# One fixed order for all five engines: a planner that orders by due times replaced by a written table

## The chip, the cores and the metric

The kernel runs on one core of a Trainium2 chip. The metric is device time in microseconds (us); lower is better. Inputs and output are float32 in device memory; the kernel computes in float16 with float32 accumulation.

## The reference

Retention (a linear attention with a decay per head) over four sequences, and then a two-layer network with GELU on its output:

```python
# q, k, v: (B=4, H=8, S=768, D=64)
gamma = 1 - 2 ** (-5 - arange(H))
for t in range(S):
    state = gamma * state + outer(k[t], v[t])          # per batch and head, 64 x 64
    y[t]  = q[t] @ state / 8
x   = y.transpose(0, 2, 1, 3).reshape(3072, 512)       # tokens x (heads * 64)
out = gelu_tanh(x @ w_in) @ w_out                      # w_in 512 x 2048, w_out 2048 x 512
```

## The kernel before

The sequence is cut into six chunks of 128 positions. A chunk holds four batches `b` = 0 to 3, so 512 tokens. All work is named by chunk and batch or by chunk and part.

**Attention of a chunk**, on the tensor engine (PE), per batch: `T` transposes the scaled q and k (L211; from chunk 3 on, q is transposed by DVE instead), `A` makes the 128 by 128 products of k and q (L220), `Yc` adds what the state of the chunks before contributes (L239), `Y` the products with v (L251), and `S` the new state (L262). Between them DVE and ScalarE (ACT) take results out of PSUM: `evT` (a copy), `evA` (times a mask, L271), `evY` (the chunk's `x`, L278 or a copy), `evS` (the state, L283). Before that, q, k and v of a batch are cast or scaled from float32 to float16 (L161, L159, L176), on ACT, DVE or GpSimd (POOL). The scaling of v from chunk 2 on is one instruction for each batch, on POOL or DVE.

**The network.** For chunk 0 and 1, `M1` is the plain product with `w_in` (L357), GELU on ACT (L373), and for chunk 0 `M2` the plain product with `w_out` (L515, 16 pieces of four matmuls of 512 columns). From there on both products use seven block products in place of eight (`m1w` L492, `m2w` L504): they need sums of halves of the operands (L394): `xs` (four sums of the chunk's x, on POOL), `gs` (16 sums of the activations, on POOL or DVE, tile `s_g`) and sums of the weights (DVE, once). Results in PSUM are combined by ACT copies (`snap`, L159) and DVE additions (`add`, L394).

**Order.** The first 34 us are written out by hand: chunk 0's attention, with `spin` matmuls on zeros (L135) where PE has nothing, then M1 of chunk 0. Chunk 0's M1 runs as three pairs of weight columns over batches 0 and 1, then 2, then 3, and ten full-width pieces of 512 columns. The weights are loaded by GpSimd's queue, four parts of `w_in` and four of `w_out`, each 512 KB as it lands in float16. In the hand-written part:

```python
    load_w_in(0)
    prep1(PO, "k", 0, 2)
    for i in range(1, 4):
        load_w_in(i)
    prep1(PO, "k", 0, 3)
    prep1(PO, "q", 0, 3)
    for i in range(NO):
        load_w_out(i)
```

Everything after that is put in order by a greedy planner inside the kernel: every operation has its needs, the engines that may run it with a duration for each (`KIND`), and a slack; at each step the planner starts the operation that can start first on any engine by its own clock. PE's work stands in four threads (attention, two of M1, M2). Engines execute their instructions in the order in which they were emitted, so the planner's choice is final. PSUM's eight banks are handed out in that order too.

The loads of q, k and v come through the queues of SyncE (SP) and ACT. Those of chunk 1 are held back until the GELU of piece 12 of M1 of chunk 0.

Of the kernel before, what the change touches and what calls it, by code (L numbers as in the profile page):

```python
# [12 lines left out]
ALU = mybir.AluOpType  # L13


@with_exitstack
def kernel(
# [9 lines left out]
    nc = tc.nc  # L27
# [93 lines left out]
    load1(nc.sync, "k", 0, 2)  # L121
    load1(nc.sync, "q", 0, 3)
    load1(nc.sync, "v", 0, 3)

# [7 lines left out]
    def spin(n):  # L132
        ps = bank("h", shape=(128, 512), name="spin_ps")
        for _ in range(n):
            nc.tensor.matmul(  # L135
                out=ps, lhsT=zero[:, 0:128], rhs=zero, start=True, stop=True
            )
# [180 lines left out]
    def o_S(b, tag="att"):  # L318
        pss["S", b] = bank(tag, shape=(128, NHP, 64), name="s_ps")
        mm_s(0, b, pss["S", b])  # L320

    def o_evS(b, eng=nc.vector):
        copy_on(eng, st_of(b), pss.pop(("S", b)))


# [48 lines left out]

    def moe1(c, fc):
        h_ps = bank("h", shape=(128, B * C), name="h_ps")
        moe1_mm(c, fc, h_ps, 0, B * C)
        gelu(g_tile(c, fc)[:, fc % 2], h_ps)

    def moe1_two(c, fp, t0, t1):  # L380

        h_ps = bank("h", shape=(128, 2, B * C // 2), name="h_ps")
        for r in range(2):
            moe1_mm(c, 2 * fp + r, h_ps[:, r, 0:t1 - t0], t0, t1)
        gelu(g_tile(c, 2 * fp)[:, :, t0:t1], h_ps[:, :, 0:t1 - t0])
# [145 lines left out]
    load1(AC, "q", 0, 2)  # L531
    load1(AC, "v", 0, 2)
    spin(14)
    prep1(VE, "q", 0, 0)
    prep1(PO, "k", 0, 0)
    prep1(AC, "v", 0, 0)
    o_T(0)
    o_evT(0, AC)
    load1(AC, "k", 0, 3)
# [4 lines left out]
    o_evA(0)  # L544
    o_T(1)
# [4 lines left out]
    o_S(0, "o")  # L550
    o_evY(0, AC)
    prep1(VE, "q", 0, 2)

    load_w_in(0)
    prep1(PO, "k", 0, 2)
    for i in range(1, 4):
        load_w_in(i)
    prep1(PO, "k", 0, 3)
    prep1(PO, "q", 0, 3)
    for i in range(NO):  # L560
        load_w_out(i)
    o_A(1)
    o_evA(1)
    spin(3)
    o_T(2)
    o_evT(2, AC)
    spin(2)
    o_Y(1)
    o_S(1, "o")
    o_evY(1, AC)  # L570
    prep1(AC, "v", 0, 2)
    spin(2)
    o_A(2)
    o_evA(2)
    o_evS(0, AC)
    prep1(AC, "v", 0, 3)
    o_evS(1, AC)
    spin(6)
    o_T(3)
    o_evT(3)  # L580


    t01, t2, t3 = (0, half), (half, half + C), (half + C, 2 * half)
    moe1_two(0, 0, *t01)
    o_A(3)
    o_evA(3)
    o_Y(2)
    o_S(2)
    o_evY(2, AC)
    moe1_two(0, 1, *t01)  # L590
    o_evS(2)
    moe1_two(0, 0, *t2)
    moe1_two(0, 1, *t2)
    o_Y(3)
    o_S(3)
    o_evY(3)
    o_evS(3)
    moe1_two(0, 2, *t01)
    for fp in range(2):
        moe1_two(0, fp, *t3)  # L600
    moe1_two(0, 2, half, 2 * half)

    raw["q", 1, 0] = tile_of(*LD1[0], shape=SIZE["ld"][1])
    ld_at["q", 1, 0] = LD1.pop(0)
    for fc in range(6, NF):
        moe1(0, fc)
        if fc == 12:
            nc.scalar.copy(out=raw["q", 1, 0][0:1, 0, 0:1], in_=g_tile(0, 10)[0:1, 0, 0:1])
    for bs in ((0, 1), (2, 3)):
        for b in bs:  # L610
            load1(SY, "q", 1, b)
            load1(SY, "k", 1, b)
        for b in bs:
            load1(SY, "v", 1, b)
    nc.sync.dma_start(out=dec.rearrange("p h t -> p (h t)"), in_=dec_h.ap())

    ENG = {"ACT": AC, "DVE": VE, "POOL": PO, "SP": SY}
    KIND = {
        "gelu": {"ACT": (0.51, 0.60)},
        "snap": {"ACT": (0.51, 0.59)},  # L620
        "add": {"DVE": (0.62, 0.70)},
        "evA": {"DVE": (0.61, 0.69)},
        "evY": {"DVE": (0.61, 0.69)},
        "evY1": {"ACT": (0.51, 0.59), "DVE": (0.61, 0.69)},
        "evS": {"DVE": (1.10, 1.20)},
        "evT": {"DVE": (0.62, 0.69), "ACT": (0.92, 1.01)},
        "cast": {"ACT": (0.53, 0.62), "POOL": (0.58, 0.62)},
        "cast2": {"ACT": (1.06, 1.15), "POOL": (1.18, 1.22)},
        "trq": {"DVE": (0.60, 0.69)},
        "evTk": {"DVE": (0.36, 0.44), "ACT": (0.50, 0.58)},  # L630
        "loadq": {"SP": (8.6, 0.0)},
        "scale": {"POOL": (1.00, 1.05), "DVE": (0.68, 0.75)},
        "scale1": {"POOL": (1.00, 1.05), "DVE": (0.68, 0.75)},
        "sumg": {"POOL": (1.12, 1.16), "DVE": (0.35, 0.42)},
        "sumx": {"POOL": (1.12, 1.16)},
        "sumw": {"DVE": (0.35, 0.42)},
        "sume": {"POOL": (1.12, 1.16), "DVE": (0.35, 0.42)},
        "load": {"SP": (0.90, 0.0)},
        "store": {"SP": (0.80, 0.0)},
    }  # L640
    LAT_PE, LAT, SAFE, AHEAD = 0.28, 0.07, 1.5, 0.4
    tok, T = {}, {}
    slots = {p: [0.0] * n for p, (n, _, _) in SIZE.items()}
    slots["bank"] = [0.0] * 8
    held_by = {}
    free_at = {"PE": 34.2, "ACT": 34.7, "DVE": 25.0, "POOL": 21.0, "SP": 47.5}
    landed = [48.6, 49.6, 51.5, 52.4]
    port = [0.0]
    todo, by_need = [], {}

    class Op:
        def __init__(self, kind, emit, needs, gives, alloc=(), free=(), slack=1.0, early=(), kb=0):
            self.kind, self.emit, self.needs, self.gives = kind, emit, needs, gives
            self.alloc, self.free, self.slack, self.early, self.kb = alloc, free, slack, early, kb

    def shared(o, e):

        return e == "POOL" or e == "DVE" and o.kind[:3] in ("sum", "sca")

    def op(*a, **k):  # L660
        todo.append(Op(*a, **k))

    def when(needs):
        t = 0.0
        for n in needs:
            if n not in tok:
                return None
            t = max(t, tok[n])
        return t

    def room(alloc):

        t, seen = 0.0, {}
        for off, (key, *_) in alloc:
            seen.setdefault(key[0], []).append(off)
        for p, offs in seen.items():
            at = sorted(x for x in slots[p] if x is not None)
            if len(at) < len(offs):
                return None
            t = max(t, max(a - o for a, o in zip(at, sorted(offs))))  # L680
        return t

    def take(alloc):
        for key, readers, *shape in alloc:
            p = key[0]
            i = min((x, i) for i, x in enumerate(slots[p]) if x is not None)[1]
            if p == "lq" and key[2] in BLK:
                i = key[3]
            slots[p][i] = None
            held_by[key] = [p, i, readers, 0.0]  # L690
            T[key] = bank_tile(i, *shape) if p == "bank" else tile_of(p, i)

    def give_back(keys, t):
        for key in keys:
            h = held_by[key]
            h[2] -= 1
            h[3] = max(h[3], t)
            if h[2] == 0:
                slots[h[0]][h[1]] = h[3]

    def finish_op(o, e, s):
        busy, lat = KIND[o.kind][e]
        free_at[e] = s + busy
        end = s + lat + LAT
        if shared(o, e):
            port[0] = s + busy
        if e == "SP":
            begin = max(landed[-1], s + 1.3)
            landed.append(max(begin + 1.15 * o.kb / 256, s + busy + 1.8 if o.kind == "loadq" else 0.0))
            end = landed[-1] + SAFE  # L710
            free_at[e] = max(free_at[e], landed[-4] if o.kind == "load" else 0.0)
        take(o.alloc)
        o.emit(ENG[e])
        for n in o.early:
            tok[n] = s
        for n in o.gives:
            tok[n] = end
        give_back(o.free, end)


    def ld_key(c, b, nm):
        early = c == 2 and b < 2 and nm != "v" or c in BLK and nm == "q"
        return ("lq" if early else "ld", nm, c, b)

    def q_cast(c, b):
        key = ("qk16", c, b)

        def emit(eng):
# [8 lines left out]
           alloc=[(key, 2 if c + 1 == NCk else 3)], early=[("al", key)], free=[("lq", "q", c, b)], slack=2.0)  # L737

        def tr(eng):
# [7 lines left out]
           early=[("al", "qkT", c, b)], free=[key], slack=1.5)  # L747

    def q_load(c):
# [3 lines left out]
        def emit(eng):  # L753
# [8 lines left out]
           early=[("issued", key)], slack=3.0, kb=1024)  # L762
        prev[0] = ("issued", key)

    def cast_in(c, b, nm):
# [4 lines left out]
        ldk = ld_key(c, b, nm) if c > 1 else ("ld", nm, c, b)  # L770
# [8 lines left out]
        if nm == "v":  # L779
            kind = "cast" if c < 2 else "scale"  # L780
        elif kind == "scale":
            kind = "scale1"
# [7 lines left out]
            slack=8.0 if nm == "v" else 2.0,  # L790
        )

    prev = [None]
# [14 lines left out]
    def sub(cost, emit, needs=(), gives=(), alloc=(), free=()):  # L808
        return (cost, emit, list(needs), list(gives), list(alloc), list(free))

    def att(c):
        units = []

        def T1(b):
# [498 lines left out]
```

## Time and profile before

| What | Value |
|---|---|
| Time, median of 3 runs | 204.42 us (204.28 to 204.44) |
| The profiled execution | 204.52 us, its span 202.7 us, so 1.8 us lie outside the span |
| Granted TensorE clock | 0.998 |
| PE busy | 192.5 us (95%) |
| DVE busy | 150.5 us (74%) |
| ACT busy | 126.6 us (62%) |
| POOL busy | 96.6 us (48%) |

A span is the time from the first to the last instruction. A busy share is an average over stages; PE also counts as busy on `spin` matmuls, which compute nothing. The tables by stretch of time that follow tell more than these shares.

### The profile page before, as it was taken

Reading aid. Unit: us, or ns where it says so; the run is one execution under the profiler, and the core shown is the slowest. Engines: PE = TensorE matmul, PEld = TensorE weight load, DVE = VectorE, ACT = ScalarE, POOL = GpSimd, SP = SyncE. Lnnn points to the kernel's source line nnn. Section 1 sums busy time; section 2 is a strip of 40 time slices with the busy share of each in tenths; the row PEclk is TensorE's granted clock in tenths of the full one; section 3 lists DMA queues with packets and bytes.
Section 4 is the critical chain, followed back from the end, with each engine's and each line's share of the span. In section 5 each row is a group of like instructions: output and inputs, shape, how many; then the busy total and the mean of one; then the engine's idle time right before and its main releaser. Section 6 shows DMA issues by size and latency. Waiting matters only on the chain. (4 is left out here: it accounts for less than half of the span.)

```text
span 202.7 us, 5761 instructions
## 1 busy us (share of the span) xinstructions
PE 192.5 (95%) x2376; PEld 153.1 (76%) x2376; DVE 150.5 (74%) x283; ACT 126.6 (62%) x235; POOL 96.6 (48%) x96
## 2 busy tenths in 40 slices
PE   7769999999999997999999999999999999999993
PEld 3336744455898885889889878789888888888883
DVE  4435585739787998997799998799995793297720
ACT  2482466053589547749948849948859916499421
POOL 0697000011202876852999903498914799241400
PEclk9999999999999999999999999999999999999999
DMA  7999999989998799968990669990002300020205
GB/s 165 287 263 206 209 204 218 224 196 247 206 229 169 116 251 217 224 109 152 250 254 12 117 98 188 228 259 2 3 0 84 127 3 3 0 103 25 83 4 204
DMA packets 95898, 30.10 MB, mean 148 GB/s; under 512 B 88320, under 2 KB 92800, under 8 KB 95872
## 3 DMA queue, kind: packets, MB, share of 16 engines
q1 hardware_dynamic: 85120, 23.45, 49.7%
q0 software_dynamic: 4224, 4.19, 12.5%
q10 hardware_dynamic: 6528, 2.10, 4.1%
q8 instruction: 18, 0.29, 0.6%
q14 instruction: 8, 0.07, 0.1%
HBM read 27.64 MB, written 6.29 MB: 167 GB/s over the span
## 5 line engine op out<-in xcount | busy, mean ns | idle before, releaser
L394 DVE TENSOR_TENSOR st<-ps,st 128x512 f32<-128x512 f32 x48 | 31.3, 681 | 9.4 <-PE ps L492 3.6
L504 PEld LDWEIGHTS <-s_g 128*128 128x128 f16 x320 | 30.8, 98 | 5.1 <-DVE s_g L394 0.8
L159 ACT COPY st<-ps 128x512 f32<-128x512 f32 x48 | 26.4, 602 | 13.0 <-PE ps L492 12.8
L373 ACT ACTIVATE g<-st 128x512 f16<-128x512 f32 x48 | 29.9, 649 | 7.3 <-DVE st L394 7.3
L492 PEld LDWEIGHTS <-w_in 128*128 128x128 f16 x256 | 24.7, 98 | 3.9 <-issue 0.6
L271 DVE TENSOR_TENSOR a<-ps,mask 128x512 f16<-128x512 f32 x40 | 24.8, 680 | 3.3 <-PE ps L220 3.3
L357 PEld LDWEIGHTS <-w_in 128*128 128x128 f16 x232 | 20.8, 98 | 7.7 <-issue 0.7
L394 POOL TENSOR_TENSOR s_g<-g 128x512 f16<-128x512 f16 x17 | 19.9, 1184 | 13.9 <-ACT g L373 13.9
L394 POOL TENSOR_TENSOR s_g<-g,s_g 128x512 f16<-128x512 f16 x15 | 17.8, 1191 | 16.2 <-DVE s_g L394 16.1
L159 ACT COPY o<-ps 128x512 f32<-128x512 f32 (+1 forms) x28 | 14.8, 529 | 17.0 <-PE ps L504 14.1
L504 PEld LDWEIGHTS <-g 128*128 128x128 f16 x240 | 23.1, 98 | 3.0
L373 ACT ACTIVATE g<-ps 128x512 f16<-128x512 f32 x32 | 19.3, 602 | 5.6 <-PE ps L357 5.4
L492 PEld LDWEIGHTS <-u_w 128*128 128x128 f16 x192 | 18.5, 98 | 3.0 <-issue 0.6
L504 PE MATMUL ps<-t_w,s_g 128*128 128x256 f16 x160 | 18.9, 273 | 1.2 <-ACT o L159 0.7
L504 PE MATMUL ps<-w_out,s_g 128*128 128x256 f16 x160 | 19.6, 273 | 0.0
L504 PE MATMUL ps<-w_out,g 128*128 128x256 f16 x160 | 19.3, 273 | 0.0
L492 PE MATMUL ps<-xs,w_in 128*128 128x256 f16 x128 | 18.6, 273 | 0.4 <-DVE st L394 0.4
L394 POOL TENSOR_TENSOR s_g<-s_g,g 128x512 f16<-128x512 f16 x10 | 11.9, 1187 | 14.8 <-DVE s_g L394 14.7
L394 DVE TENSOR_TENSOR o<-ps,o 128x512 f32<-128x512 f32 (+1 forms) x18 | 10.7, 593 | 9.6 <-PE ps L504 9.6
L492 PE MATMUL ps<-xs,u_w 128*128 128x256 f16 x128 | 16.6, 273 | 0.5 <-DVE a L271 0.5
L492 PE MATMUL ps<-x,w_in 128*128 128x256 f16 x128 | 16.3, 273 | 0.0
L357 PE MATMUL ps<-x,w_in 128*128 128x256 f16 x128 | 15.3, 273 | 0.1
(73 smaller groups left out, 320.6 us busy)
## 6 DMA issues: line engine op xcount, KB each, us to landing
ld<-in_v_dram SPq DMA_DIRECT2D x19, 256.0 KB, 4.4
ld<-in_k_dram SPq DMA_DIRECT2D x17, 256.0 KB, 5.3
out_dram<-o SPq DMA_DIRECT2D x8, 512.0 KB, 3.8
ldq<-in_q_dram SPq DMA_DIRECT2D x48, 64.0 KB, 2.8
w_in<-in_moe_w_in_dram POOLq DMA_DIRECT2D x4, 512.0 KB, 9.4
w_out<-in_moe_w_out_dram POOLq DMA_DIRECT2D x4, 512.0 KB, 14.4
ld<-in_q_dram SPq DMA_DIRECT2D x5, 256.0 KB, 4.6
out_dram<-o SPq DMA_DIRECT2D x5, 256.0 KB, 3.0
```

Source lines behind the costliest of these rows:

```text
L159: eng.copy(out=out, in_=in_)
L271: eng.tensor_tensor(out=a_sb[c, b, j], in0=ps, in1=mask[:, j], op=ALU.mult)
L357: nc.tensor.matmul(out=out, lhsT=w_in_sb[wi][:, kc, wr * 128:(wr + 1) * 128], rhs=xT[c][:, kc, t0:t1], start=(kc == 0), stop=(kc == NHP - ...
L373: nc.scalar.activation(out=out, in_=in_, func=AF.Gelu_apprx_tanh, scale=1.0)
L394: eng.tensor_tensor(out=out, in0=in0, in1=in1, op=op)
L492: nc.tensor.matmul(out=ps[:, f], lhsT=m1_lhs(lk, kc, 2 * g + f), rhs=x[:, kc], start=(n in FIRST and kc == 0 and f == 0), stop=(n in (1, 5 ...
L504: nc.tensor.matmul(out=ps, lhsT=m2_lhs(c, lk, fp, a), rhs=m2_rhs(rk, fp), start=(first and fp == 0), stop=(n in (1, 5, 6) and fp == NP - 1 ...
```

## The change

The planner, its slacks, its due times and its threads are removed. All operations are numbered in the order in which the program makes them, and a table `ORDER` of words says in which order they are emitted: the letter is the engine (p PE, a ACT, v DVE, g POOL, s SP), the number is the operation. `w2` is a pair of spin matmuls. A loop emits them:

```diff
+    for at, word in enumerate(ORDER.split()):
+        e, i = word[0], int(word[1:])
+        if e == "w":
+            ps = bank_tile(min(x for x in slots["bank"] if x is not None)[1], (128, 512), name="spin_ps")
+            spin_on(ps, i)
+            continue
+        o = items.pop(i)
+        assert e in KIND[o.kind] and done.issuperset(o.needs), (word, o.needs)
+        take(o.alloc)
+        o.emit(by[e])
+        done.update(o.early, o.gives)
+        give_back(o.free, 1000.0 + at)
+    assert not items
```

The table begins:

```
g7 g0 p169 v168 a8 p179 w2 p172 v171 v170 v9 g1 p181 g2 p185 a184 p191 a190 p193 a180 p183
a182 a192 a178 p195 p197 a194 a196 p207 p209 p211 a210 a206 v10 g3 g4 v136 v137 v144 p174
p213 v173 p215 p217 p177 g5 v176 v175 a11 p189 a208 v152 v160 p199 a212 a198 v188 a216 p201
p187 a186 p203 p205 a202 a204 p219 a218 p221 a220 g6 s12 s13 s14 s15 s16 v161 p223 p225 p227
```

Read out, PE's first words are: T of batch 2, S of batch 0, two spins, A of batch 2, S of batches 1 and 2, then `p191`, the first piece of M1 of chunk 0, a second piece, Y of batch 2, two more pieces, three half-width pieces for batch 2, T of batch 3, and so on. POOL's first words are: scale k of batch 2 (`g7`), trigger `w_in` part 2 (`g0`), part 3 (`g1`), `w_out` parts 0 to 2 (`g2` to `g4`), part 3 (`g5`), and `g6`, which holds the loads of chunk 1.

M1 of chunk 0 now has 24 pieces: for each of eight pairs of weight columns one over batches 0 and 1 (matmuls of 256 columns), one over batch 2 and one over batch 3 (128 columns):

```diff
+    def m1_first():
+        for t0, t1, bs, cost, kind in ((0, half, (0, 1), 0.873, "gelu"), (half, half + C, (2,), 0.45, "gelu2"),
+                                       (half + C, 2 * half, (3,), 0.45, "gelu2")):
+            for fp in range(NP):
```

The weight triggers stand between scalings. Parts 0 and 1 of `w_in` come right after the first scaling of k on POOL; the others are words of the table, three of them behind a scaling of batch 2 or 3, and the loads of chunk 1 behind the last trigger and a GELU:

```diff
     prep1(PO, "k", 0, 0)
+    load_w_in(0)
+    load_w_in(1)
     prep1(AC, "v", 0, 0)
...
+    def trig(nm, i, n):
+        load = load_w_in if nm == "win" else load_w_out
+        behind = {2: [("k16", 0, 2)], 3: [("q16", 0, 3)], 5: [("k16", 0, 3)]}.get(n, [])
+        op("trig", lambda eng: load(i), [("trig", n - 1)] + behind, [(nm, i)], early=[("trig", n)], cost=LANDS[n])
+
+    def hold():
+        T["lq", "q", 1, 0] = tile_of("lq", 0)
+
+        def emit(eng):
+            eng.tensor_copy(out=T["lq", "q", 1, 0][0:1, 0, 0:1], in_=misc[0:1, 0:1])
+
+        op("hold", emit, [("trig", 7), ("H0", 7, 0)], ["held"])
```

The scaling of k and q of batch 3 moves from POOL to DVE, and the loads of batches 2 and 3 of chunk 0 go, all but one, through SP's queue:

```diff
-    load1(nc.sync, "k", 0, 2)
-    load1(nc.sync, "q", 0, 3)
-    load1(nc.sync, "v", 0, 3)
-
+    load1(nc.scalar, "q", 0, 2)
+    for at in (("k", 2), ("v", 2), ("q", 3), ("k", 3), ("v", 3)):
+        load1(nc.sync, at[0], 0, at[1])
```

Which engine runs what changes with the table too. In the table, POOL has 14 scalings of v (7 in the trace before) and DVE 2 (9 before); POOL has 48 of the `s_g` sums (42 before) and DVE 32 (38 before).

In the middle of the table, for chunk 3, POOL's words from the last `xs` sum of chunk 2 (`g355`) on are scalings of v, `s_g` sums and casts up to `g476`; that one, `g478`, a cast, `g477` and `g479` are the `xs` sums of chunk 3 with a cast between them. Between `g355` and `g476` stand 11 `s_g` sums, 6 scalings of v and 3 casts. The first product that reads one of the four is `p504`. The last Y of chunk 2 is `p349`.

## The prediction

> **What bounds the kernel now.** I read the busy shares first, then busy time by stretch, then PE's timeline where it shows gaps, then the DMA queues in the first stretch.
>
> The page says that PE bounds:
>
> ```profile
> span 202.7 us, 5761 instructions
> PE 192.5 (95%) x2376; PEld 153.1 (76%) x2376; DVE 150.5 (74%) x283; ACT 126.6 (62%) x235; POOL 96.6 (48%) x96
> ```
>
> The view by stretches, cut at the first M1 matmul (17.87 us) and around PE's gaps, says where PE is not fed (columns: length, then busy us of PE, PEld, DVE, ACT, POOL, clock, DMA):
>
> ```profile
> 17.87:24.60 6.73, 6.25 (x105) 5.26 (x106) 4.17 (x9) 3.31 (x7) 1.01 (x2) 1.00 1.24 206
> 24.60:77.00 52.40, 52.29 (x619) 36.09 (x620) 39.97 (x79) 29.09 (x51) 12.52 (x12) 1.00 0.98 206
> 77.00:81.00 4.00, 2.65 (x73) 2.10 (x70) 3.50 (x6) 3.18 (x6) 2.41 (x4) 1.00 0.99 223
> ...
> 115.00:119.00 4.00, 3.53 (x33) 3.01 (x32) 4.00 (x5) 1.41 (x3) 1.78 (x2) 1.00 0.56 87
> ...
> 130.00:133.00 3.00, 2.58 (x66) 1.98 (x63) 2.08 (x4) 2.68 (x6) 1.59 (x2) 1.00 1.15 250
> ...
> sum 181.83, PE 178.98 PEld 146.47 DVE 143.15 ACT 118.12 POOL 85.92; mean PE 22.37 PEld 18.31 DVE 17.89 ACT 14.77 POOL 10.74
> ```
>
> From 17.87 to 199.70 PE idles only 181.83 - 178.98 = 2.85 us: 0.48 in the first stretch, 1.35, 0.47 and 0.42 at three joints between chunks, the rest in crumbs. The clock is 1.00 throughout. So there are two things to win: start M1 sooner, and close the joints (2.24 us). The start, in PE's timeline:
>
> ```profile
> 14.61 0.32 PE L262 MATMUL s_ps<-v,qk 128*64 128x64 f16 x8 [1.60 <-ACT st L159]
> 14.86 0.61 PE L135 MATMUL spin_ps<-zero 128*128 128x512 f16 x2
> 15.40 0.42 PE L220 MATMUL a_ps<-qkT 64*64 64x128 f16 x16
> 15.75 1.47 PE L135 MATMUL spin_ps<-zero 128*128 128x512 f16 x6
> 17.05 0.61 PE L211 MATMUL qkT_ps<-iden,qk 128*128 128x128 f16 x8
> 17.87 1.05 PE L357 MATMUL h_ps<-x,w_in 128*128 128x256 f16 x8 [0.20 <-DMA w_in<-in_moe_w_in_dram]
> ```
>
> PE spins and waits until the first weights land. They were triggered at 9.01 (0.94 us on POOL), yet in the DMA view of 9.5 to 13.2 us only the loads of q, k and v move:
>
> ```profile
> q1 hardware_dynamic: 2154, 0.54, 65.0%
> q10 hardware_dynamic: 2080, 0.52, 62.8%
> ```
>
> The weights' queue q0 is absent there. It runs afterwards at 206 GB/s, so a part of 0.524 MB takes 2.55 us.
>
> **Term 1, M1 starts sooner.** Parts 0 and 1 are now triggered after POOL's first scaling of k, which ended at 6.44, so at 6.45 in place of 9.01. Both triggers (0.94 + 0.80) go ahead of the scaling of k of batch 1, which moves from 7.83 to 8.2. T, A and Y of batch 1 and its x move with it: the x of batch 1 was copied at 13.18 to 13.77 and now ends at 14.1. ACT then casts v of batch 2 (0.63: 14.75), on which S of batch 2 waits; it is the last word before `p191`. T of batch 2 (0.45) ends at 13.65, its copy on DVE (0.69) at 14.55, A (0.35) at 14.95, S of batch 1 and 2 at 15.2. So PE is ready at 15.2.
>
> Are the weights? If the queues serve in order of issue, nine loads of 0.262 MB and 0.11 MB of constants go first, 2.47 MB at 287 GB/s (5 to 10 us) from 1.7 us: 10.3; one more load makes it 11.2. Then 2.55 us for the part, and the time to be seen: part 0 landed 8.4 us after 9.01, at 17.4, where its data began at 13.2 and took 2.55, so 1.65 more. That gives 14.5 to 15.4, about when PE is ready. The other bound is that q0 waits until all q, k and v loads are through, as in the view above: 17.9, no gain. I take 15.2, since every load that went first in the trace had also been issued before 9.01. Term: 15.2 - 17.87 = -2.67. The Trainium skill (DMA: Bandwidth & Descriptors, Queues, rings and completion order) says that a DMA engine takes turns between the queues with work, packet by packet. By that rule q0 should have moved data between 11 and 13.2, which the row does not show; here it would bring part 0 to about 14 and change nothing, since PE is ready at 15.2.
>
> **Term 2, work moved behind the start.** T of batch 3 (0.45) goes behind, S of batch 2 (0.22) in front. M1 of chunk 0 had 40 matmuls of 512 columns (8.63 us), 32 of 256 (3.49) and 32 of 128 (1.78): 13.90. It becomes 64 of 256 (8 x 0.873 = 6.98) and 128 of 128 (16 x 0.445 = 7.12): 14.10. A change of the array's form costs 0.09: 24 matmuls of 256 columns and their change at 52.12 take 2.71 against 3 x 0.873 = 2.62. The name of the change suggests fewer of these. I counted them in the order of the timeline and in the table: 46 behind the M1 start before, 50 now, +0.37. Term: 0.45 - 0.22 + 0.20 + 0.37 = +0.80. ACT has 24 GELUs in chunk 0 (8 x 0.60 + 16 x 0.38 = 10.9 us for 9.9); it was busy 3.31 of 6.73 there, so they hide.
>
> **Term 3, idle in the first stretch.** Part 1 is usable at 15.0 + 2.55 = 17.5; PE comes to `p195` at 15.2 + 2 x 0.873 + 0.45 = 17.4. Two late loads (0.9 each) come between, so part 2 is usable at 21.9; PE comes to `p215` at 21.5. Part 3 (24.5) is early for 25.8. I allow 0.9 where 0.48 was: +0.4. The bounds are 0 and 2 (a late v of batch 3 blocks ACT's cast `a11`, and the GELUs queued behind it hold PSUM banks). The loads of chunk 1 are released by a GELU at about 27.5 and not at 32.4; PE then has M1 for batch 3 and ten pieces of M2 to do, until about 40, and the DMA total is the same, so I cost their move at nothing. If that cover were gone PE would stand for about one load and its landing, 0.9 + 1.65.
>
> **Term 4, the joints.** DVE was full at 115 to 119 (4.00 of 4.00). Seven scalings of v (7 x 1.04) and six `s_g` sums (6 x 0.60) leave it: -10.9. POOL gains 7 x 1.22 + 6 x 1.19 = 15.7. Chunk 3's joint, from the end of `p349`: DVE does a state update and two evictions (1.08 + 2 x 0.68 = 2.4), then POOL four `xs` sums (4.8), 11 `s_g` sums (13.1), 6 scalings (7.3), 3 casts (1.9) and the first `xs` sum of chunk 3 (1.2): 30.7, with semaphores 30.9. PE from there to `p504`: 31 pieces of m1w (13.5), 16 of m2w (14.0), attention 4.1, eight form changes 0.8: 32.4. So POOL has 1.5 us to spare. I allow 0.4 for each of three joints, 1.2, for 2.24 and 0.13 in crumbs: -1.1. The bounds are 0 and 3.
>
> **Sum.** -2.67 + 0.80 + 0.4 - 1.1 = -2.6 on the profiled 204.52 (span 202.7 and 1.8 outside), which is 0.1 above the median 204.42: 201.9. A measurement here can tell about 0.2% (0.4 us) from no change.
>
> **Rivals.**
> *POOL becomes the bound (slower).* The place is POOL between `g355` and `g476`, the price what it exceeds its spare, and it decides from 1.5 us, 5% of 30.9. For it: POOL's sums wait for others' results. In the list of groups:
>
> ```profile
> L394 POOL TENSOR_TENSOR s_g<-g 128x512 f16<-128x512 f16 x17 | 19.9, 1184 | 13.9 <-ACT g L373 13.9
> L394 POOL TENSOR_TENSOR s_g<-g,s_g 128x512 f16<-128x512 f16 x15 | 17.8, 1191 | 16.2 <-DVE s_g L394 16.1
> L394 POOL TENSOR_TENSOR s_g<-s_g,g 128x512 f16<-128x512 f16 x10 | 11.9, 1187 | 14.8 <-DVE s_g L394 14.7
> ```
>
> That is 44.9 us of idle before 42 sums, 1.07 each. If a third of it stays, 11 sums lose 3.9, 2.4 beyond the spare, at the joints of chunks 3 and 4: +4.8, 206.7. Against it: POOL idled there because it ran out of ready work. DVE's sums cost 0.60 on average beside POOL and 0.42 with POOL idle (L394 into `u_w` and `s_g`). The Trainium skill (SBUF — State Buffer, two separate sides) calls the port that GpSimd and VectorE share an exclusive lock, also against a VectorE operation with two SBUF inputs. By that rule more POOL work makes both wait for whole instructions; the 0.60 against 0.42 agrees. Chance 0.17.
>
> *The weights are no sooner (the change doesn't do that).* q0 waits for all q, k and v loads: M1 at 17.9, term 1 gone: 201.9 + 2.67 = 204.6, no change. Chance 0.10.
>
> *Loads block in-order queues.* A fixed order cannot step round a late load: 3 us in the first 30 us or for chunk 2: 204.9. For it: DMA is busy (0.98 to 65 us). Chance 0.07.
>
> **How the numbers follow.** The forecast has 0.66; its own range is 199.8 (terms 3 and 4 without idle) to 203.7 (the worse of the two at its upper end). Low is 199.5. High is 206.2: it takes in the two middle rivals and the lower half of POOL's, and leaves out under 2 in 10. Faster 0.68 (forecast and a mild form of the third rival), same 0.08 (most of the late weights), slower 0.24 (POOL's 0.17, the rest of the others).
>
> **What would show it.** Term 1: the first L357 at 15.2, with q0 moving before q1 has done. Term 2: about 50 form changes. Term 3: gaps of PE under 1 us between 15 and 30, put down to `w_in`. Term 4: three joints under 0.5 us, DVE's v scalings down to 2. I am wrong if L357 still starts near 17.9, or if L492 on `xs` waits for POOL by over 1 us at a joint, or if gaps put down to loads of q, k or v appear before 65 us.

## The result and the profile after

The changed kernel takes 218.53 us (median of 4 runs, 217.69 to 219.83) against 204.43 for the kernel before on the same chip: a ratio of 1.068 with a 95% interval of 1.061 to 1.075. The forecast of 201.9 and its range to 206.2 were wrong, and on the wrong side. The profiled execution took 218.76, with a span of 217.0; it is 14.2 us longer than the profiled one of before (204.52). Some executions fall into a slower state whatever the kernel is, and the times of the experiments are medians without them.

From the page of the changed kernel:

```profile
span 217.0 us, 5902 instructions
PE 197.5 (91%) x2458; PEld 160.2 (74%) x2458; DVE 144.1 (66%) x274; ACT 123.1 (57%) x232; POOL 113.3 (52%) x114
PEclk9996795699999999999999999999999999999999
```

PE stood idle for 19.5 us of the span, where it was 10.2 before, and its busy time rose by 5.0 us. The clock row says where: in four of the five slices from the fourth to the eighth (each 5.4 us long) the granted clock is at 0.5 to 0.7, and nowhere else. The view by stretches shows the same in us (length, then busy PE, PEld, DVE, ACT, POOL, clock, share of the DMA engines, GB/s):

```profile
15.00:20.00 5.00, 0.23 (x10) 0.22 (x7) 1.10 (x2) 0.62 (x1) 1.10 (x3) 0.80 1.22 197
20.00:25.00 5.00, 5.00 (x36) 3.28 (x33) 0.00 (x0) 1.89 (x5) 0.00 (x0) 0.51 1.22 196
25.00:30.00 5.00, 3.01 (x42) 2.70 (x39) 0.69 (x1) 2.46 (x6) 0.00 (x0) 1.00 1.21 196
30.00:35.00 5.00, 1.91 (x19) 1.91 (x20) 2.39 (x5) 0.00 (x0) 0.00 (x0) 0.67 1.22 196
35.00:40.00 5.00, 2.91 (x40) 2.34 (x39) 2.57 (x6) 1.18 (x3) 0.00 (x0) 0.50 1.07 216
...
47.60:213.10 165.50, 164.47 (x2108) 137.46 (x2105) 123.64 (x226) 107.14 (x202) 100.67 (x97) 1.00 0.50 117
```

From 15 to 20 us all engines are nearly empty at once while the DMA share is over 1, and from 25 to 35 us none is busy for more than 3.01 of 5 us: everybody waits for data. From 47.6 us on PE idles 1.03 us in 165.5. M2 begins at 47.64 where it began at 34.09, and from there to the end of the span the two kernels need 169.4 and 168.6 us. So 13.5 of the 14.2 us are lost before M2 begins. PE's timeline of that stretch:

```profile
14.70 0.32 PE L319 MATMUL ps<-v,qk 128*64 128x64 f16 x8
19.78 0.43 PE L319 MATMUL ps<-v,qk 128*64 128x64 f16 x8 [4.77 <-ACT v L216]
20.14 3.60 PE L406 MATMUL ps<-x,w_in 128*128 128x256 f16 x16
...
33.09 0.61 PE L268 MATMUL ps<-iden,qk 128*128 128x128 f16 x4 [5.08 <-DVE qk L233]
...
38.92 0.42 PE L319 MATMUL ps<-v,qk 128*64 128x64 f16 x8 [2.09 <-ACT v L216]
```

PE waits 4.77 us for the cast v of batch 2, 5.08 for the scaled k of batch 3 and 2.09 for v of batch 3: 11.94 together. The weights are not what it waits for. One step back, ACT's and DVE's timelines name what those casts waited for:

```profile
19.11 0.62 ACT L216 CAST v<-ld 128x512 f16<-128x512 f32 x1 [5.54 <-DMA ld<-in_v_dram]
32.34 0.69 DVE L233 TENSOR_TENSOR qk<-ld,cst 128x512 f16<-128x512 f32 x1 [5.96 <-DMA ld<-in_k_dram]
38.26 0.62 ACT L216 CAST v<-ld 128x512 f16<-128x512 f32 x1 [9.77 <-DMA ld<-in_v_dram]
```

The loads of chunk 0 come late. The last four (each 1024 packets) had all their packets through at 16.5, 23.2, 29.9 and 36.4 us, 6.5 to 6.7 us apart; in before all were through by 13.4. Each was used 1.9 to 2.6 us after that, when the last of its 16 landing events had come: for v of batch 2, fifteen came from 17.45 to 17.90 and one at 19.09. SP, POOL and the DMA queues say why:

```profile
11.45 10.72 SPq L164 DMA_DIRECT2D ld<-in_v_dram  x1
```
```profile
11.47 1.55 POOL L387 DMA_DIRECT2D w_in<-in_moe_w_in_dram  x2
13.00 2.98 POOL L396 DMA_DIRECT2D w_out<-in_moe_w_out_dram  x4
15.93 0.18 POOL L752 COPY ldq<-misc 1x1 f32<-1x1 f32 x1
```
```profile
q0 software_dynamic: 2997, 2.97, 91.5%
q1 hardware_dynamic: 2997, 0.76, 29.9%
```

The last fence is the queues from 15.9 to 35 us (packets, MB, share). Each queue moved 2997 packets: they take turns, one packet each. A packet of the weights is 1024 B and one of the loads 256 B, so q0 lands 155 GB/s and the loads 40, where the loads alone ran at 287. POOL had issued all eight weight parts by 16 us, because nothing held it: the table's "needs" of a trigger order only when it is emitted, and POOL's rows show that nothing on the chip waits for them. In before the triggers of `w_out` had stood behind POOL's own scalings of batch 3, and a scaling cannot start before its load has landed. The change moved the two to DVE (`v9`, `v10`).

**Theory A**: the weights starve the loads of chunk 0, and three edits together allow it: early triggers of parts 0 and 1, the scalings of q and k of batch 3 taken from POOL, all late loads on one queue, which holds one turn in two. **Rivals**: B, the table's new order or POOL's extra work costs the time; C, PE's clock, low after each gap, costs it.

### The profile page after: what moved, and what is told of

The parts are those of the page before. It is cut to its first block, busy times and chain, and to the rows that moved or that the text cites. A ratio compares the mean times of both kernels' runs of the same rounds, so it can differ in the third digit from the quotient of the medians.

```text
span 217.0 us, 5902 instructions
## 1 busy us (share of the span) xinstructions
PE 197.5 (91%) x2458; PEld 160.2 (74%) x2458; DVE 144.1 (66%) x274; ACT 123.1 (57%) x232; POOL 113.3 (52%) x114
## 4 chain that ended last, share of the span: by engine, by line
PE 50%; DVE 0%; ACT 0%; issue 0%
PE ps L541 25%; PE ps L529 20%; PE ps L277 2%; PE ps L308 1%; PE ps L268 1%; PE ps L296 1%; PE ps L319 0%; DVE st L431 0%; ACT o L216 0%
## 5 line engine op out<-in xcount | busy, mean ns | idle before, releaser
L422 ACT ACTIVATE g<-ps 128x512 f16<-128x512 f32 (+1 forms) x56 | 28.2, 540 | 12.3 <-PE ps L406 10.0
L406 PE MATMUL ps<-x,w_in 128*128 128x256 f16 (+1 forms) x320 | 35.0, 273 | 0.0
L431 POOL TENSOR_TENSOR s_g<-g 128x512 f16<-128x512 f16 x22 | 25.9, 1183 | 15.6 <-ACT g L422 15.6
L328 DVE TENSOR_TENSOR a<-ps,mask 128x512 f16<-128x512 f32 x44 | 27.9, 683 | 6.3 <-PE ps L277 5.9
L406 PEld LDWEIGHTS <-w_in 128*128 128x128 f16 x320 | 28.5, 107 | 4.8 <-issue 0.2
L529 PEld LDWEIGHTS <-w_in 128*128 128x128 f16 x256 | 24.4, 98 | 4.9 <-issue 1.6
L431 POOL TENSOR_TENSOR s_g<-s_g,g 128x512 f16<-128x512 f16 x14 | 16.3, 1171 | 7.9 <-DVE s_g L431 7.4
L529 PE MATMUL ps<-x,w_in 128*128 128x256 f16 x128 | 17.4, 272 | 0.9 <-DVE st L431 0.9
L218 POOL CAST v<-ld 128x512 f16<-128x512 f32 x2 | 3.4, 1704 | 28.5 <-DMA ld<-in_v_dram 28.5
L529 PE MATMUL ps<-xs,u_w 128*128 128x256 f16 x128 | 18.1, 273 | 0.0
L431 POOL TENSOR_TENSOR s_g<-g,s_g 128x512 f16<-128x512 f16 x12 | 14.8, 1250 | 2.3 <-DVE s_g L431 2.3
```

The costliest lines, as they stand in the source:

```text
L218: eng.tensor_copy(out=out, in_=in_)
L328: eng.tensor_tensor(out=a_sb[c, b, j], in0=ps, in1=mask[:, j], op=ALU.mult)
L406: nc.tensor.matmul(out=out, lhsT=w_in_sb[wi][:, kc, wr * 128:(wr + 1) * 128], rhs=xT[c][:, kc, t0:t1], start=(kc == 0), stop=(kc == NHP - ...
L422: nc.scalar.activation(out=out, in_=in_, func=AF.Gelu_apprx_tanh, scale=1.0)
L431: eng.tensor_tensor(out=out, in0=in0, in1=in1, op=op)
L529: nc.tensor.matmul(out=ps[:, f], lhsT=m1_lhs(lk, kc, 2 * g + f), rhs=x[:, kc], start=(n in FIRST and kc == 0 and f == 0), stop=(n in (1, 5 ...
```

## The experiments

**e1, the gate put back.** Two words of the table:

```diff
-... v171 v170 v9 g1 p181 ... a206 v10 g3 g4 ...
+... v171 v170 g9 g1 p181 ... a206 g10 g3 g4 ...
```

> Theory A (starved loads): GpSimd's triggers wait for nothing, because the two scalings that stood before them now run on DVE; all eight weight parts are queued by 16 us, the DMA engines serve the weights' queue and SP's queue one packet each in turn (1024 B against 256 B), and the last loads of chunk 0 land at 19 to 38 us. Giving the scalings of q and k of batch 3 back to GpSimd makes the triggers of part 3 and of w_out wait again: only three parts then compete, batch 3 lands by about 24 us and not 38, and the time falls by 8 to 10 us to 208 to 211; M1 still starts near 20 us, because v of batch 2 competes with parts 0 to 2. Rival B (the table's order itself is slow, whatever the triggers do): 216 to 219. Rival C (the fall of PE's clock is the cost): 212 to 215.

Measured: 207.29 us, just under the range, ratio 1.016 (1.010 to 1.022). POOL now stands where it should, in its timeline:

```profile
21.88 1.03 POOL L233 TENSOR_TENSOR qk<-ld,cst 128x512 f16<-128x512 f32 x1 [9.58 <-DMA ld<-in_q_dram]
```

The last five parts are triggered at 22.87 and after, the last load of chunk 0 is through at 22.1 instead of 36.4, and some 11 us are back. What is left is mostly one wait of 4.51 us ahead of M1, for v of batch 2, since parts 0 and 1 are still early.

**e2, parts 0 to 2 later as well** (e1 with part 0 behind POOL's second scaling, parts 1 and 2 at the word `g0`):

```diff
     prep1(PO, "k", 0, 0)
-    load_w_in(0)
-    load_w_in(1)
...
     prep1(PO, "k", 0, 1)
+    load_w_in(0)
```

> As e1, and parts 0 to 2 of w_in are triggered where they were before (part 0 behind the scaling of k of batch 1, parts 1 and 2 behind that of batch 2). Theory A: no load is starved, M1 starts at about 17.9 us, PE's clock stays at 1.0, and the time is 203 to 206 us (the prediction's sum without its first term is 204.6). Rival B: over 210 us, with the gaps of PE behind 25 us.

Measured: 205.48, ratio 1.003 (1.000 to 1.005). The time is as expected, M1's start is not: 15.98, not 17.9, because q0's first packet came at 11.76, and not after the loads. The gain is spent at once: PE waits 2.54 us at 20.8 for part 1, triggered at 11.68.

**e8, the triggers late and the scalings left on DVE** (the change with e2's edit to the triggers, without e1's two words):

> The changed kernel with only its early triggers undone (part 0 behind the scaling of k of batch 1, parts 1 and 2 behind that of batch 2); the scalings of batch 3 stay on DVE, so part 3 and w_out follow at once. Theory A: 0.57 MB of loads are left when the weights begin at 12 us and go at 39 GB/s, so v of batch 3 lands near 27 us; PE gets there at about 26 anyway (e2): 206 to 209, most of the 14 us gone by this one edit as well. Rival: the lost gate alone is the cost, so over 213.

Measured: 205.66, just under the range, ratio 1.004 (1.001 to 1.008). v of batch 3 was through at 16.7 and not near 27 as expected: until 16.3 q0 had moved part 0 alone. So undoing the early triggers alone takes back 12.9 us, undoing the scalings alone some 11. The two do not add up: here the loads of chunk 0 are through before most of the weights move, and in e1 only three parts compete with them.

**e3, the kernel before with all triggers early.** If A holds, before must become slow by the triggers alone, with no table in it:

```diff
     prep1(PO, "k", 0, 0)
+    for i in range(4):
+        load_w_in(i)
+    for i in range(NO):
+        load_w_out(i)
...
-    load_w_in(0)
     prep1(PO, "k", 0, 2)
-    for i in range(1, 4):
-        load_w_in(i)
...
-    for i in range(NO):
-        load_w_out(i)
```

> The kernel before with one edit: all eight weight triggers right behind the first scaling on GpSimd. Theory A: chunk 0's last loads share with the weights from about 10 us on; two queues (SP's and ACT's) get a packet each per packet of the weights, some 80 GB/s in place of 288, so the 1.15 MB that are left land by about 24 us and not 13.5; M1 stands behind T of batch 3 and starts near 25 us: 210 to 214 us. Rival B: early triggers cost nothing, 203 to 205.

Measured: 212.91, ratio 1.040 (1.037 to 1.044). The last loads of chunk 0 are through at 20.8 and 25.6, M1 starts at 23.9. Time and start are as expected, but in part by luck, for POOL's and PE's timelines show a second cause that the expectation did not have:

```profile
6.73 3.17 POOL L338 DMA_DIRECT2D w_in<-in_moe_w_in_dram  x4
9.87 3.00 POOL L347 DMA_DIRECT2D w_out<-in_moe_w_out_dram  x4
12.83 1.11 POOL L176 TENSOR_TENSOR qk<-st,cst 128x512 f16<-128x512 f32 x1
```
```profile
13.99 0.61 PE L211 MATMUL qkT_ps<-iden,qk 128*128 128x128 f16 x4 [4.23 <-POOL qk L176]
...
29.67 1.11 PE L357 MATMUL h_ps<-x,w_in 128*128 128x128 f16 x16 [2.94 <-ACT x L159]
```

The eight triggers hold POOL for 6.1 us, so the scaling of k of batch 1 comes at 12.83 (7.83 in before) and PE waits 4.23 us for it. That wait is POOL's issuing and no starved load. The wait of 2.94 is one: ahead of it ACT stood 6.79 us for v of batch 3. So e3 shows that early triggers delay the loads without any table, which rival B does not have; of its 8.1 us only a part is starvation.

**e4, the clock.** Matmuls on zeros put into the three gaps of the changed kernel (`w20`, `w22`, `w9` ahead of `p185`, `p174`, `p189`):

> The changed kernel with spin matmuls put where PE stood (20 before S of batch 2, 22 before T of batch 3, 9 before S of batch 3), so that its clock has no reason to fall. Theory A: the waits for loads stay, only matmuls at half clock get faster: 214.5 to 217 us. Rival C (the clock is most of the cost): under 209 us.

Measured: 217.27, ratio 1.061 (1.059 to 1.064), with a clock of 1.00 over the whole span. The last load is through as late as in the change (36.4); the lost clock was worth about 1.3 us by the medians, and the intervals of the two ratios overlap. Rival C falls as the main cause. The time is just above the range that A gave: I had priced the clock at 1.5 to 4.

**e5 and e6, two attempts at a good order with one load queue.** Both start from e1 and make the hold real (it reads a GELU's output, so that the loads of chunk 1 wait for it):

```diff
-in_=misc[0:1, 0:1]
+in_=g_tile(0, 14)[0:1, 0, 0:1]
```

e5 has parts 0 and 1 behind POOL's second scaling:

> As e1 (scalings of batch 3 on GpSimd), with parts 0 and 1 triggered together behind the scaling of k of batch 1, and the hold of chunk 1's loads made to read an element of the GELU that it was meant to wait for. Theory A (packets of the weights and of the loads share in turn, and every trigger that waits for nothing costs): in e2 PE stood 2.5 us for part 1, triggered at 11.7, and chunk 1's loads took packets from the weights from 22 us on; both go, so 203 to 204 us, about 2 less than e2 (205.5). Rival D (what is left against the forecast of 201.9 lies in the table's later order): 205 to 206.

Measured: 210.74, ratio 1.029 (1.025 to 1.032), a miss by 7 us. q of batch 3 happened to land early (11.6), which opened the gate in front of part 3 and the first `w_out` part at 13.5; k and v of batch 3 then took turns with five parts and were through at 19.7 and 26.3. PE waited for one of the parts and then for v of batch 3, and behind each wait its clock was at 0.5 for 3.4 us:

```profile
19.33 4.92 PE L406 MATMUL ps<-x,w_in 128*128 128x256 f16 x40 [1.88 <-DMA w_in<-in_moe_w_in_dram]
...
29.33 0.32 PE L319 MATMUL ps<-v,qk 128*64 128x64 f16 x8 [2.94 <-ACT v L216]
```

The weights suffer from the loads as the loads do from the weights. A gate on one load protects that load, not those issued behind it.

e6 has part 0 at 6.4 and part 1 behind the second scaling:

> As e5, but part 0 alone is triggered at 6.45 us, as in the change, and part 1 behind the scaling of k of batch 1. Theory A: one part takes the turn of about 0.13 MB of loads, so v of batch 2 comes some 2.5 us later than in e5 but before 16; M1 starts at 15.2 to 16, later waits grow by up to 1: 202.5 to 204.5. Rival (any early part starves the loads): over 205.

Measured: 206.5, ratio 1.010 (1.006 to 1.013), a miss as well. v of batch 2 was through at 13.6, S of batch 2 waited 2.58 us for its cast, and M1 started at 18.16. With one load queue, one early part is enough to delay a load on which PE's next step hangs.

**e7, all three edits undone.** e5 with v of batch 2 and k of batch 3 on ACT's queue, as in before:

```diff
-    for at in (("k", 2), ("v", 2), ("q", 3), ("k", 3), ("v", 3)):
+    for at in (("k", 2), ("q", 3), ("v", 3)):
...
+    load1(AC, "v", 0, 2)
     spin(14)
...
     o_evT(0, AC)
+    load1(AC, "k", 0, 3)
```

> As e5, with v of batch 2 and k of batch 3 of chunk 0 loaded through ACT's queue, at the places that the kernel before had for them. Theory A: where both load queues have work they get two packets per packet of the weights, so batch 3 lands 2 to 4 us sooner and parts 0 and 1 up to 1 us later: 202.5 to 204.5, within 1 us of e5. Rival (SP's single queue was the cause of the late loads): 2 us or more under e5.

Measured: 204.04, ratio 1.000 (0.997 to 1.002). All loads are through at 13.5, q0's first packet is at 13.30, M1 starts at 18.31 and no wait over 0.7 us follows. Theory A had it within 1 us of e5; it is 6.7 below, and 2 or more was the sign that SP's single queue counts. So the number of load queues is part of the cause. This is the table's order with loads and triggers much as in before (and with e5's real hold), and it costs nothing: rival B falls.

**e12, the change with the load queues alone undone.**

> The change itself (218.5 us) with one part undone: v of batch 2 and k of batch 3 of chunk 0 are loaded again on ScalarE's queue q10, as in before, in place of all on SyncE's q1. Triggers stay early and ungated, and the scalings of batch 3 stay on VectorE. If the load of one queue is what each turn carries, two load queues get two of three packets: a round of 98 + 18 + 18 ns moves two load packets where 98 + 18 ns moved one, so the four loads that took 6.7 us each in the change (26.8 us) take about 15.5, and the last load of chunk 0 lands at 25 to 26 instead of 36.4. TensorE's waits before 40 us (11.9 us) fall to 5 to 7, and the time is 211 to 214. If the number of load queues does not matter (the weights take the DMA engines whatever queues the loads stand in), the last load still lands after 33 and the time is 216 to 219.

Measured: 207.76, ratio 1.013 (1.007 to 1.018): 10.8 us below the change. The last load is through at 25.7, as expected, and PE's waits fall to the low end of what was expected: 1.58 us for a weight and 3.45 for v of batch 3, 5.0 together. But the time is 3 us below the range. The expectation counted waits alone; PE's busy time fell too, from 197.5 to 193.9, as no slice of the granted clock is under 0.8. The queues from 15.9 to 20 us:

```profile
q0 software_dynamic: 551, 0.55, 78.6%
q1 hardware_dynamic: 555, 0.14, 26.0%
q10 hardware_dynamic: 552, 0.14, 15.7%
```

Three queues take equal turns, so with a second load queue the loads move two packets of three in place of one of two: 69 GB/s instead of 40. M1 starts at 15.97, 0.8 us later than the change was to bring.

**e11, the prediction's first term by itself** (e9, below, with part 0 at 6.3):

> e9 with part 0 of w_in triggered ahead of GpSimd's second scaling (about 6.4 us, as in the change) and all else held: the first term of the prediction by itself, with the loads on two queues. If the queues serve in the order of issue, as the prediction's sum had it, M1 of chunk 0 starts at about 15.2 instead of 18.3, no load of chunk 0 lands later than 16, and the time is 2 to 3 us below e9: 200 to 201. If the weights take turns with the loads packet by packet, q0 moves from about 10, the last load of chunk 0 lands at 16 to 19 instead of 13.5, TensorE waits 2 to 4 us for scaled q, k or v before M1, and the time is 1 to 5 us above e9: 204 to 208.

Measured: 206.00, ratio 1.004 (1.000 to 1.008), 2.6 us above e9. In PE's timeline:

```profile
15.06 1.92 PE L406 MATMUL ps<-x,w_in 128*128 128x256 f16 x16
...
19.49 3.26 PE L406 MATMUL ps<-x,w_in 128*128 128x256 f16 x40 [2.17 <-DMA w_in<-in_moe_w_in_dram]
...
24.37 0.40 PE L268 MATMUL ps<-iden,qk 128*128 128x128 f16 x4 [1.39 <-POOL qk L233]
```

M1 starts at 15.06, within 0.2 us of the forecast. But q0 moved from 10.53 in turns with the loads, part 1 had landed only at 19.44, the last loads were through at 21.1 and 22.0 (16 to 19 had been expected), and PE gave the time back in two waits of 2.17 and 1.39, both behind the start of M1 and not ahead of it.

**e9 and e10, the tail, and a version that beats both.** In the change 3.99 us lie between the end of the last matmul (213.01) and the end of the span, in before 3.02. ACT's timeline of the change has one row with both of its last stores behind its last copy; before had issued each of the two ahead of a copy. e9 is e7 with the last words put so:

```diff
-a948 v942 a951 s943 v945 s946 s949 s952
+v942 s943 a948 s949 a951 v945 s946 s952
```

> The kernel of e7 (two load queues, scalings of batch 3 on GpSimd, triggers behind a real wait; 204.0 us) with the last words of the table reordered, so that ScalarE's two last stores are issued between its two last copies, as before did, and not both behind them. In all table kernels the span ends 4.0 to 4.2 us behind the last matmul, in before 3.0. If the two late stores are the reason (five stores of 128x256 floats then land almost together), the distance falls to 3.0 and the time to 202.8 to 203.3 us. If the distance has another reason, it stays at 4.1 and the time at 203.8 to 204.3.

Of the change first, then of e9:

```profile
213.05 0.85 ACTq L562 DMA_DIRECT2D out_dram<-o  x2
```
```profile
195.41 0.37 ACTq L562 DMA_DIRECT2D out_dram<-o  x1
...
197.11 0.36 ACTq L562 DMA_DIRECT2D out_dram<-o  x1
```

Measured: 203.43, ratio 0.997 (0.995 to 0.999). The distance fell to 3.56, about half of what was expected; the other half is not explained. The ratio's interval overlaps e7's, so the tail's share of the time is likely but not settled; that e9 is faster than before is.

> e9 with eleven matmuls on zeros ahead of M1 of chunk 0 (11 x 0.26 us = 2.9 us, in place of the 3.06 us in which TensorE stands before the first w_in part lands). In e7 the first 16 matmuls of M1 took 3.29 us where 16 of them take about 1.7 at full clock. If the lost clock is a price of the gap, the time is 1.0 to 1.8 us below e9, so 201.2 to 202.2. If the matmuls on zeros only take the place of the wait and the clock costs nothing behind it, it equals e9 within 0.3 us.

Measured: 203.64, ratio 0.995 (0.993 to 0.997), not to be told from e9. In e9's profiled execution the first 16 matmuls of M1 took 1.92 us where e7's took 3.29: the wait ahead of them was 1.56 there, not 3.06. So there was little for the added matmuls to save, and in e10 they are what M1 waits for:

```profile
15.36 2.55 PE L192 MATMUL spin_ps<-zero 128*128 128x512 f16 x11
17.96 0.32 PE L319 MATMUL ps<-v,qk 128*64 128x64 f16 x8
18.21 1.92 PE L406 MATMUL ps<-x,w_in 128*128 128x256 f16 x16
```

M1 of e7 and e9 began at 18.31 and 16.64, as soon as the last of part 0's 16 landing events had come (18.26 and 16.60). The other fifteen lie close together in both (to 16.91 and 16.55). What delays the one in e7 is not settled.

## Why the prediction was wrong

**The step that failed is in term 1**: "If the queues serve in order of issue". I read the absence of q0 between 9.5 and 13.2 as waiting in line. As far as the runs show it was the time that q0 takes to start: its first packet came 2.3 to 4.3 us after the start of the first trigger in every run here (6.45 to 9.67 in the change, 8.94 to 11.76 in e2, 6.73 to 10.58 in e3, 9.01 to 13.30 in before). In before the loads were over just when q0 came up. Moved 2.6 us forward, q0 came up among the loads, and so it did in e3, e11 and e12 with two load queues. The reason given for 15.2, that every load had been issued before the trigger, did not carry over either: with the trigger at 6.45, SP issued the loads of batch 3 at 7.65, 9.45 and 11.45. The rule that I quoted from the Trainium skill (DMA: Bandwidth & Descriptors, Queues, rings and completion order), that an engine takes turns packet by packet, I set aside because "the row does not show" it; here 2997 packets against 2997 show it to the packet. And I asked only what the rule does for the weights ("change nothing"), not what it does to the loads they meet: that was the decisive question.

**The terms.** Term 1 gave -2.67. PE's side of it was sound: where loads and weights share well enough (e11, e12) M1 starts at 15.06 and 15.97 against 15.2. But in the change "ACT then casts v of batch 2 (0.63: 14.75)" became 19.73, as that load had lost its turns, and M1 started at 20.14: +2.3 in place of -2.67.

Term 3 allowed 0.4 us and at most 2 for idle time in the first stretch; 7.17 came behind M1's start (5.08 and 2.09) and 4.77 ahead of it. The bound of 2 was taken from one late v. I took loads for finished that were still queued: the change put five of them on SP's queue, whose issues before had taken 1.76 us each and now stood up to 10.72. I also took the table's needs for waits: "released by a GELU at about 27.5" is an order of emission, and POOL ran the hold at 15.93.

Term 2 (+0.80): PE's busy time from M1's start to its last matmul is 178.98 in before, 179.19 in e9 and 179.30 in e10, all at a clock of 1.00: +0.2 to +0.3. The form changes were counted well (50, as forecast); the size was too high by 0.5, and which part of it is not settled.

Term 4 (-1.1, to 1.2 of idle at the joints): gaps after 70 us sum to 0.94 in the change, 0.93 in e7, 0.67 in e9 and 1.63 in e10, against 2.24: 0.6 to 1.6 less, so the term is about right. DVE's 38 sums of before took 21.3 us, 0.56 each and not the 0.60 of the prediction, which changes little. POOL as the bound did not come: its busy time rose from 96.6 to 113.3, but its sums' idle time fell from 44.9 to 25.8 us, in the groups of the change:

```profile
L431 POOL TENSOR_TENSOR s_g<-g 128x512 f16<-128x512 f16 x22 | 25.9, 1183 | 15.6 <-ACT g L422 15.6
L431 POOL TENSOR_TENSOR s_g<-s_g,g 128x512 f16<-128x512 f16 x14 | 16.3, 1171 | 7.9 <-DVE s_g L431 7.4
L431 POOL TENSOR_TENSOR s_g<-g,s_g 128x512 f16<-128x512 f16 x12 | 14.8, 1250 | 2.3 <-DVE s_g L431 2.3
```

The sum had no term for the stores at the end: +0.97.

**The rival that came** is the third, "Loads block in-order queues", with its place right and its size wrong: 3 us instead of 12 in waits and about 1.3 in clock. It was priced as a mishap of one load; it is a rate, 40 GB/s instead of 287 for as long as weights are queued, and so it grows with what is still to be loaded. The sign I had named for it (gaps put down to loads of q, k or v before 65 us) is what the profile shows.

**What each edit is worth.** From 218.53: one load queue undone, 207.8; scalings of batch 3 undone, 207.3; early triggers undone, 205.7; all three undone (and the hold made real), 204.0; the tail as well, 203.4. Undoing any one takes back most, so the full loss needs all three. That one alone is cheap is not shown: with late triggers, POOL's scalings and one load queue, e2 took 205.5 and e5 210.7.

## What to carry to other kernels

When a transfer is triggered earlier, list every transfer that is still to land at that moment and what the next steps of the critical engine need of it: here queues shared by packets, so the queue with packets of 1024 B took most of the bandwidth from the one with 256 B (155 to 40 GB/s), and the number of queues on each side is a knob. Before taking a step from an in-order engine, ask what that step's wait held back behind it; an order of emission in a table is not a wait. Triggers also take the time of the engine that issues them (6.1 us for eight, in e3). A queue that is absent from a window need not be waiting in line: compare its first packet with its trigger in more than one place.

## What the runs showed of the hardware that was not expected

- Turns by packet are exact: 2997 to 2997 with two queues, 551, 555 and 552 with three, though one queue has packets of 1024 B and the others of 256. A packet of the weights took 96 ns (median), one of the loads 18 ns alone and 31 between weights; a load of 1024 packets on 16 engines is 64 turns, at 6.7 us 105 ns each.
- The first weight trigger on POOL (0.94 us of issue) shows its first packet only 2.3 to 4.3 us after its start: 2.3 to 3.3 in the kernels with the late loads on one queue, 3.4 to 4.3 in those with two. Part 1 of e2, triggered at 11.68 with part 0 through by 15.6, began only at 16.30. Why is open.
- One of a transfer's 16 landing events can come over 1 us behind the other fifteen, and the transfer counts as landed only then: 19.09 against 17.90 for v of batch 2 in the change, 18.26 against 16.91 for part 0 in e7, but 16.60 against 16.55 in e9.
- An issue on SP stood 10.72 us where such an issue took 1.76 with the queue moving; SP then ran as late as its data.
- Gaps of 4.77 and 5.08 us took the granted clock to 0.5, yet kept at 1.00 by matmuls on zeros the kernel gained only about 1.3 us; where the waits were shorter (e5) a stretch of 3.4 us at 0.5 made 40 matmuls take 4.92 us in place of 3.26.
